# Strided convolution with group norm and GELU, forward and backward: products without matmuls of zeros, five more split leaves, a finer first chunk

## The chip, the cores and the metric

The kernel runs on one core of one Trainium2 chip. The metric is the device time of one execution in microseconds (us); lower is better. The time shown is the median of three executions. One more execution was taken with the hardware profiler; the durations below are from that one.

## The reference

Two sequences of 16000 rows and 256 channels (bf16) go through a strided convolution, a normalisation over time for each sequence and channel, and GELU. The second half of the work is the gradient for all four inputs.

```python
B, T, D, K = 2, 16000, 256, 31
s = 2
L = (T - K) // s + 1                                   # 7985
h = jnp.einsum('blc,cd->bld', x[:, 0:s * L:s, :], w[0])
for i in range(1, K):
    h = h + jnp.einsum('blc,cd->bld', x[:, i:i + s * L:s, :], w[i])
mu = jnp.einsum('bld->bd', h)[:, None, :] / L
var = jnp.einsum('bld->bd', (h - mu) ** 2)[:, None, :] / L
h = (h - mu) / jnp.sqrt(var + 1e-5)
h = h * gn_gamma[None, None, :] + gn_beta[None, None, :]
out = gelu(h, approximate=True)
# reference(): out, and the gradients of x, w, gn_gamma, gn_beta for a given grad_out
```

## The kernel before

The three convolutions (forward, gradient of the input, gradient of the weights) are computed by a fast scheme in the manner of Karatsuba, nested. Tap index and time index are both split by their low bits. At each level four products are replaced by three: one of the "A" parts, one of the "C" parts, and one "B" product of differences or sums, which is added to one and subtracted from the other. Two levels give nine combinations of (branch, leaf), each out of A, B and C. A third level can be applied to a leaf; a leaf to which it is applied is called split here. A leaf that is not split is one long sum of matmuls (`f_leaf`, `g_leaf`, `w_leaf`). A split leaf has three parts: one product of a pair, which TensorE makes once and ScalarE copies to both halves of a PSUM tile with a sign (`f_three_b`, `f_outer`, `g_three_b`, `g_outer`, `w_pairs`), and two further products added on top (`f_three_ac`, `g_three_ac`, `w_single`). That takes three quarters of the matmul columns of the whole leaf, and additional sums or differences on VectorE.

**PSUM.** There are four tiles `ring[0]` to `ring[3]`, each of two banks of 512 fp32 columns. A matmul with the start flag begins a bank anew, and later matmuls into that bank add to it. In `f_three_b` and `w_pairs` the product takes only one half of each bank; one matmul of zeros (weights and data from the zero tile `zt2`) starts each bank before them, writing the other half. The product of one bank is then copied to its own other half, both banks in one ScalarE instruction (L604, L1440).

**Stages.** F is the forward pass (`forward`, matmuls recorded at L572), over 2 batches x 4 chunks x 3 branches. F0 is batch 0 and F1 is batch 1; beside F1 runs the elementwise work of batch 0 (`gelu_batch`, `gelu_unit`). G is the input gradient (`input_grad`, L1103), beside which run the elementwise work of batch 1, the preparation `e_load`, `e_comp`, `dn_turn` of each chunk's gradient, and `d2_piece`, which prepares differences of the gradient for the last stage and writes them to DRAM. W is the weight gradient (`weight_grad`, L1359): nine combinations n = 0 to 8 in turn, with the PSUM pairs X = ring[0:2] and Y = ring[2:4].

**One combination of W.** `x_tile` builds four tiles of x (two blocks of 16384 rows, called b = 0 and 1, in two halves each) by adding raw loads (`w_add`, L1322). `XSUM` is the sum of the two halves for each batch (L1322 as well), `pair_x` (L1419) adds neighbouring rows of a tile, `pair_d` (L1427) and `leaf_d` (L1483) take differences of the gradient. The B product is always split: `w_pairs` into X, then `w_single` into X. Its result seeds the A leaf (in Y) and the C leaf (in X), by a copy or by a VectorE sum with an earlier result (`ve`, L647). Then the two leaves are computed, and `w_done` stores or keeps their results (`w_emit`, L1391). A leaf is split when (n, leaf) is in `NODES`:

```python
NODES = {(0, C_), (6, A), (6, C_), (7, A), (8, C_)}
```

The pair sums of a split leaf live in the buffers `PD`. For n < 2 there are two sets ("all" and "early"), for n > 5 two ("all" and "late"), and for n = 2 to 5 only "all", which the B product uses too. `XSUM` of batch 0 and the temporary of a seed share addresses in some combinations.

**One step of F.** `f_sums` gives the operands (L540). The B leaf is always split except in the very first step. In batch 0 (the set `FO`) the outer leaves A and C are split too, with the weight differences `WD`, the ScalarE copies of `f_outer` (L637) into `TS`, and three operand buffers `U`; in batch 1 they are whole leaves. `f_seed` (L647, L651) adds the results of the B branch.

**The first chunk.** Rows of x are loaded in three pieces (`rows[0]`, `rows[1]` of 128, `rows[2]` of 16) and one half of the chunk is transposed by TensorE against an identity (`x_first`): slot by slot, each with the transposes of both large pieces; then VectorE (L495) and ScalarE (L493) copy the results out. `f_first` makes the first weight differences (`w_sub`, L530) and the first sums before the first leaf.

**Order.** Each instruction is recorded by `add` with its reads and writes and a due time. A planner (`Plan.listing`) runs a list of ready instructions per engine by due time and writes all in the resulting order. The due times follow the order of TensorE's work; `lead` shifts them by kind and stage, `slack` by a constant, `look` limits how far TensorE's groups may be exchanged, `pads` delay what depends on transfers, `hold` ties a piece to a place in TensorE's order, and `PACE` gives the due times of the elementwise units. Each engine and each DMA queue then works strictly in this order. All large transfers are issued by SyncE (SP).

Lines that the text names: L403 loads and stores, L408 DMA transposes, L530 `w_sub`, L540 sums of F, L572 matmuls of F, L604 copy of `f_three_b`, L637 copies of `f_outer`, L647 and L651 VectorE sums of seeds, L655 ScalarE copies (`keep`), L1003 and L1006 elementwise step of a chunk of gradient on VectorE, L1009 and L1011 the same on ScalarE, L1103 matmuls of G, L1266 differences in `d2_piece`, and in W L1322 `w_add`, L1359 matmuls, L1391 `w_emit`, L1419 `pair_x`, L1427 `pair_d`, L1440 copy of `w_pairs`, L1483 `leaf_d`.

Of the kernel before, what the change touches and what calls it, by code (L numbers as in the profile page):

```python
# [38 lines left out]
class Plan:  # L39
# [3 lines left out]
    def __init__(self, tc):  # L43
# [5 lines left out]
        self.slack = 20.0  # L49
        self.hold = -1  # L50
        self.look = 14
        self.pads = (582.0, 557.0, 161.0)
        self.lead = {
            "F0 f_mm f_leaf": -5.0,
            "F0 f_mm f_outer": -6.5,
            "F0 f_mm f_three_ac": -5.5,
            "F0 f_mm f_three_b": -9.0,
            "F0 f_outer forward": 7.5,
            "F0 load put": -14.0,
            "F0 tt f_sums": 7.5,  # L60
            "F0 tt third": -3.0,
            "F0 turn x_load": -10.5,
            "F0 ve f_seed": -4.5,
            "F1 f_mm f_three_ac": 4.0,
            "F1 gelu_unit gelu_batch": 1.5,
            "F1 load gelu_unit": 4.0,
            "F1 tt f_sums": 2.0,
            "F1 tt gelu_unit": -3.5,
            "F1 tt second": 4.0,
            "F1 tt third": -4.0,  # L70
            "F1 ve f_seed": 4.0,
            "G0 g_mm g_leaf": 1.0,
            "G0 g_mm g_three_ac": 1.0,
            "G0 g_mm g_three_b": 1.5,
            "G0 keep g_evac": -3.5,
            "G0 load dn_turn": -17.0,
            "G0 load e_load": 9.5,
            "G0 load g_evac": -3.5,
            "G0 load load_w2": -4.0,
            "G0 spread e_comp": 7.5,  # L80
            "G0 tiny elem_finalize": -8.0,
            "G0 turn dn_turn": 1.5,
            "G0 zero e_comp": 2.0,
            "G1 e_comp conv_stem_kernel": -6.0,
            "G1 g_mm g_leaf": -2.0,
            "G1 g_mm g_outer": 4.5,
            "G1 g_mm g_three_b": 4.5,
            "G1 g_outer input_grad": 2.5,
            "G1 keep g_evac": -2.0,
            "G1 keep g_seed": 10.0,  # L90
            "G1 load d2_piece": 1.0,
            "G1 load dn_turn": 17.0,
            "G1 load e_load": -4.0,
            "G1 load g_evac": 8.5,
            "G1 spread e_comp": -8.5,
            "G1 sub d2_piece": -2.5,
            "G1 tt first": 3.0,
            "G1 tt second": -4.5,
            "G1 turn dn_turn": -2.5,
            "G1 ve g_seed": -1.0,  # L100
# [226 lines left out]
def conv_stem_kernel(  # L327
# [1243 lines left out]
    for br in (B_, C_, A):  # L1571
        load_w2(br)
# [68 lines left out]
```

## Time and profile before

| | |
|---|---|
| median of three executions | 1219.03 us (1217.96 to 1220.42) |
| profiled execution | 1218.8 us, span 1217.0 us, granted TensorE clock 1.00 |
| busy: TensorE / VectorE / ScalarE / GpSimd | 1186.9 / 992.4 / 580.7 / 23.0 us |
| stage F, first to last matmul | 4.7 to 441 us |
| stage G | 441 to 879 us |
| stage W | 879 to 1213 us |
| DMA | 263.55 MB, 16 engines busy 76% of the span |

In the rows, PE is TensorE's matmul, PEld its weight load, DVE is VectorE, ACT is ScalarE, POOL is GpSimd and SP is SyncE. Matmuls overlap in the array, so one matmul's own duration is longer than the distance to the next. A group's row has the number of instructions after x, then the busy time and the mean duration of one in ns. Windows are in us from the span's start.

### The profile page before, as it was taken

The page shows a single profiled execution, that of the slowest core. Times are in us where ns is not written, and L with a number is a line of the kernel's source. Part 1 is how long each engine was busy: PE and PEld are TensorE (multiplying, and loading weights), DVE is VectorE, ACT ScalarE, POOL GpSimd, SP SyncE. Part 2 cuts the span into 40 slices and gives each one's busy share as a digit, 9 for nine tenths or more (in the row PEclk, how much of TensorE's full clock was granted, in tenths as well). Part 3 has the DMA queues.
Part 4 walks back from the last instruction along what each step waited for, and adds up shares of the span by engine and source line. Part 5 has one row for each costly group of instructions (what it writes and reads, how often), then busy time and mean ns, then how long its engine had stood idle before and what let it go on. Part 6 is the DMA issues. An engine that isn't in the chain of part 4 may idle for free.

```text
span 1217.0 us, 19291 instructions
## 1 busy us (share of the span) xinstructions
PE 1186.9 (98%) x7782; PEld 767.1 (63%) x7846; DVE 992.4 (82%) x1265; ACT 580.7 (48%) x801; POOL 23.0 (2%) x68
## 2 busy tenths in 40 slices
PE   6999999999999999999999999999999999999998
PEld 4888889777776974444444444444466665566865
DVE  6988787789999748999885697988785976879883
ACT  1243343478886358878776775544421121112200
POOL 1000000000000000101000000000000000000000
PEclk9999999999999999999999999999999999999999
DMA  9457638758976987685735799998899798897562
GB/s 207 71 158 143 163 96 171 181 130 193 207 188 163 315 296 179 207 241 161 231 117 153 198 323 312 289 336 268 285 249 337 230 322 274 265 334 248 180 177 65
DMA packets 344931, 263.55 MB, mean 217 GB/s; under 512 B 187068, under 2 KB 324538, under 8 KB 336570
## 3 DMA queue, kind: packets, MB, share of 16 engines
q1 hardware_dynamic: 344586, 262.31, 75.7%
q8 instruction: 61, 1.00, 0.3%
q14 instruction: 28, 0.23, 0.1%
q0 software_dynamic: 256, 0.00, 0.0%
HBM read 129.44 MB, written 87.52 MB: 178 GB/s over the span
## 4 chain that ended last, share of the span: by engine, by line
PE 83%; DVE 6%; ACT 4%; DMA 4%; issue 2%; SPq 0%; another core or an unknown queue 0%; POOL 0%; DVEq 0%; ACTq 0%; POOLq 0%
PE ps L572 28%; PE ps L1103 28%; PE ps L1359 26%; DMA arena<-in_x_dram 2%; DVE arena L530 2%; ACT arena L675 1%; DVE arena L540 1%; DVE arena L1266 1%; DMA arena<-dnd 1%; DMA d2d<-arena 1%; DVE arena L914 1%; DVE ps L647 1%; ACT arena L688 1%; ACT arena L1009 1%; DVE arena L647 0%
## 5 line engine op out<-in xcount | busy, mean ns | idle before, releaser
L572 PE MATMUL ps<-arena 128*128 128x256 bf16 (+4 forms) x3552 | 425.3, 281 | 15.4 <-DMA arena<-in_x_dram 9.0
L1103 PE MATMUL ps<-arena 128*128 128x512 bf16 (+1 forms) x1975 | 429.8, 376 | 5.4 <-DVE ps L647 2.1
L572 PEld LDWEIGHTS <-arena 128*128 128x128 bf16 x3552 | 346.9, 98 | 92.8 <-issue 10.7
L1103 PEld LDWEIGHTS <-arena 128*128 128x128 bf16 x2016 | 197.4, 98 | 237.1 <-issue 6.3
L1359 PE MATMUL ps<-arena 128*128 128x256 bf16 (+1 forms) x2153 | 331.6, 313 | 2.0 <-DVE arena L1483 0.5
L655 ACT ACTIVATE arena<-ps 128x1024 f32<-128x1024 f32 (+1 forms) x143 | 145.6, 1020 | 302.3 <-PE ps L1359 76.8
L1359 PEld LDWEIGHTS <-arena 128*128 128x128 bf16 x2176 | 212.9, 98 | 113.4 <-issue 1.2
L540 DVE TENSOR_TENSOR arena<-arena 128x1088 bf16<-128x1088 bf16 (+3 forms) x194 | 163.2, 882 | 14.5 <-PE ps L572 14.2
L914 DVE TENSOR_TENSOR arena<-arena 128x1024 bf16<-128x1024 bf16 x160 | 106.7, 685 | 14.0 <-ACT arena L906 7.9
L1322 DVE TENSOR_TENSOR arena<-arena 128x4096 bf16<-128x4096 bf16 x42 | 95.5, 2285 | 25.3 <-PE ps L1359 18.4
L647 DVE TENSOR_TENSOR ps<-ps,arena 128x1024 f32<-128x1024 f32 x77 | 93.5, 1225 | 27.1 <-PE ps L1359 11.7
L1062 DVE TENSOR_TENSOR arena<-arena 128x516 bf16<-128x516 bf16 (+3 forms) x176 | 82.3, 507 | 10.9 <-PE ps L1103 10.7
L675 ACT ACTIVATE arena<-ps 128x512 bf16<-128x512 f32 (+1 forms) x64 | 37.0, 580 | 87.7 <-PE ps L572 87.6
L1266 DVE TENSOR_TENSOR arena<-arena 128x768 bf16<-128x768 bf16 (+3 forms) x112 | 65.9, 636 | 10.9 <-DMA d2d<-arena 5.6
L647 DVE TENSOR_TENSOR ps<-arena,ps 128x1024 f32<-128x1024 f32 x43 | 52.6, 1224 | 11.5 <-ACT arena L637 4.6
L1483 DVE TENSOR_TENSOR arena<-arena 128x2304 bf16<-128x2304 bf16 x36 | 47.9, 1349 | 13.2 <-PE ps L1359 13.2
L1440 ACT COPY ps<-ps 128x512 f32<-128x512 f32 x28 | 16.0, 572 | 83.7 <-PE ps L1359 83.7
L647 DVE TENSOR_TENSOR arena<-arena 128x1024 f32<-128x1024 f32 x32 | 38.8, 1220 | 15.1 <-ACT arena L1140 7.2
L904 DVE SCALAR_TENSOR_TENSOR arena<-arena 128x1024 bf16<-128x1024 bf16 x32 | 39.0, 1218 | 7.1 <-ACT arena L902 7.0
L530 DVE TENSOR_TENSOR arena<-arena 128x2048 bf16<-128x2048 bf16 (+1 forms) x45 | 42.3, 979 | 0.7 <-DMA arena<-vl 0.7
L924 ACT ACTIVATE arena<-arena 128x1024 bf16<-128x1024 bf16 x32 | 33.6, 1050 | 15.3 <-DVE arena L914 15.3
L900 ACT ACTIVATE arena<-arena,stats 128x1024 bf16<-128x1024 bf16 x32 | 39.3, 1229 | 2.0 <-issue 1.2
(81 smaller groups left out, 627.7 us busy)
## 6 DMA issues: line engine op xcount, KB each, us to landing
arena<-in_x_dram SPq DMA_DIRECT2D x52, 1024.0 KB, 10.3
arena<-d2d SPq DMA_DIRECT2D x16, 1216.0 KB, 11.5
out_dram<-arena SPq DMA_DIRECT2D x14, 1024.0 KB, 5.4
d2d<-arena SPq DMA_DIRECT2D x30, 384.0 KB, 4.8
arena<-dnd SPq DMA_DIRECT2D x10, 960.0 KB, 8.7
vl<-arena SPq DMA_DIRECT2D x36, 256.0 KB, 2.5
arena<-vl SPq DMA_DIRECT2D x9, 1024.0 KB, 8.0
hd<-arena SPq DMA_DIRECT2D x8, 1024.0 KB, 6.0
```

The source lines that it names most:

```text
L530: add("DVE", dve(n), [o], [a, b], lambda: nc.vector.tensor_tensor(out=o, in0=a, in1=b, op=ALU.subtract))
L540: lambda: nc.vector.tensor_tensor(out=o, in0=a, in1=b, op=ALU.add))
L572: yield nc.tensor.matmul(ps[:, dh, cs], lhsT=wt, rhs=mv, start=s0, stop=False, skip_group_check=True)
L647: add("DVE", dve(1024, 1), [out], [a, b], lambda: nc.vector.tensor_tensor(out=out, in0=a, in1=b, op=op))
L655: lambda: nc.scalar.activation(out=out, in_=ps, func=ACT.Copy, scale=scale))
L675: lambda o=o, i=i, ac=ac: nc.scalar.activation(out=o, in_=i, func=ACT.Copy, accum_out=ac))
L914: add("DVE", dve(1024), [o], [a, b_], lambda: V.tensor_tensor(out=o, in0=a, in1=b_, op=op))
L1062: lambda: nc.vector.tensor_tensor(out=o, in0=a, in1=b, op=ALU.add))
L1103: yield nc.tensor.matmul(ps[:, e, 0:wide], lhsT=lt, rhs=mv, start=s0, stop=False, skip_group_check=True)
L1266: lambda: nc.vector.tensor_tensor(out=out, in0=a, in1=b_, op=ALU.subtract))
L1322: add("DVE", dve(4096), [o], [a, b], lambda: nc.vector.tensor_tensor(out=o, in0=a, in1=b, op=ALU.add))
L1359: yield nc.tensor.matmul(ps[:, s, c0:c1], lhsT=lt, rhs=mv, start=s0, stop=False, skip_group_check=True)
```

## The change

Seven things change; the rest of the code is the same.

1. In `f_three_b` and `w_pairs` both halves of the product go side by side into the first bank of the PSUM tile, the first matmul with the start flag. The matmuls of zeros are gone. Three ScalarE copies of 256 columns then fill the second bank and the first bank's other half; before, it was one copy of 2 x 256. `f_outer` takes its weight differences and its temporary as arguments.
2. `NODES` gets the A leaves of n = 1 to 5.
3. In batch 1's last chunk the outer leaves of all three branches are split. Six weight differences are made for that (`f_again`) in addresses of their own.
4. The first chunk: all transposes of the first piece of x stand ahead of those of the second, the small last copy goes from VectorE to ScalarE, the first weight difference and the first sum are made in two halves, the first leaf starts with one half of its taps, and the weights are loaded in another order. The loads of gamma and beta and four stores of zeros move from the start to the second chunk.
5. The elementwise step of batch 1's first chunk moves from ScalarE to VectorE; for its other chunks ScalarE does it in halves.
6. The seven `d2_piece` of batch 0 are spread from the last chunk of batch 0 on, two at a time; before, they began with batch 1.
7. `PACE`, `slack`, `look`, `pads`, the transfer costs and the table `lead` get new values (the table is left out below).

```diff
-        self.slack = 20.0
+        self.slack = 60.0
-        self.look = 14
-        self.pads = (582.0, 557.0, 161.0)
+        self.look = 11
+        self.pads = (1348.0, 1420.5, 1031.5)
...
     def f_three_b(ps, br, lf, op, co):
+        jobs = []
         for dh in range(2):
-            jobs = [(dh, slice(HM, 512), zt2[:, 0:P], zt2[:, 0:HM], True)]
             for q2 in range(2):
                 for par in range(2):
                     for ch in range(2):
                         o0 = (2 * par + ch) * XM + co + q2
-                        jobs.append((dh, slice(0, HM), WD[br, lf][:, ch, q2, par, dh * P:(dh + 1) * P],
-                                     op[:, 1, o0:o0 + HM], False))
-            f_mm(ps, jobs, [ps[:, dh]], [WD[br, lf], op[:, 1], zt2[:]])
-        add("ACT", act(512), [ps[:]], [ps[:]],
-            lambda: nc.scalar.activation(out=ps[:, :, HM:512], in_=ps[:, :, 0:HM], func=ACT.Copy, scale=-1.0))
+                        jobs.append((0, slice(HM * dh, HM * dh + HM), WD[br, lf][:, ch, q2, par, dh * P:(dh + 1) * P],
+                                     op[:, 1, o0:o0 + HM], dh + q2 + par + ch == 0))
+        f_mm(ps, jobs, [ps[:, 0]], [WD[br, lf], op[:, 1]])
+        for o, i, sc in ((ps[:, 1, 0:HM], ps[:, 0, HM:512], 1.0), (ps[:, 1, HM:512], ps[:, 0, HM:512], -1.0),
+                         (ps[:, 0, HM:512], ps[:, 0, 0:HM], -1.0)):
+            add("ACT", act(256), [o], [i],
+                lambda o=o, i=i, sc=sc: nc.scalar.activation(out=o, in_=i, func=ACT.Copy, scale=sc))
...
     def x_first(flat, rows):
...
-        for j, slot in ((0, 2), (1, 3), (2, 0), (3, 1)):
-            ps = ring[slot]
-            for dh in range(2):
-                pe_turn(ps, dh, [(256 * (r % 2) + P * g, g, P, j, r) for r in (2 * dh, 2 * dh + 1) for g in range(2)])
+        slots = (2, 3, 0, 1)
+        for g in range(2):
+            for j in range(4):
+                for dh in range(2):
+                    pe_turn(ring[slots[j]], dh, [(256 * (r % 2) + P * g, g, P, j, r) for r in (2 * dh, 2 * dh + 1)], g == 0)
+        for j in range(4):
+            ps = ring[slots[j]]
...
-        put("DVE", flat.rearrange("p (j o r) f -> p j o r f", j=4, o=2)[:, :, 1, :, 256:XM],
+        put("ACT", flat.rearrange("p (j o r) f -> p j o r f", j=4, o=2)[:, :, 1, :, 256:XM],
...
-    FO = {(0, c, br) for c in range(NCK) for br in ORDER if c or br != B_}
+    FO = {(0, c, br) for c in range(NCK) for br in ORDER if c or br != B_} | {(1, 3, br) for br in FLAST}
...
+    def f_again():
+        zero(U[2][1][:, F - 1:F], 1, "DVE")
+        for br in FLAST:
+            for lf in (A, C_):
+                v = W[br][:, lf]
+                w_sub(WD1[br, lf], v[:, :, 1:4:2], v[:, :, 0:4:2])
...
     def f_first(xt):
         for sl in (A, C_):
             for ch in range(2):
-                w_sub(W[B_][:, sl, ch], W[C_][:, sl, ch], W[A][:, sl, ch])
+                for v in ([slice(None)] if ch or sl == C_ else [0, 1]):
+                    w_sub(*(W[br][:, sl, ch, :, v] for br in (B_, C_, A)))
...
+    EDVE = {(0, 0), (0, 1), (0, 2), (0, 3), (1, 0)}
...
-            if b == 0:
+            if (b, c) in EDVE:
...
-    NODES = {(0, C_), (6, A), (6, C_), (7, A), (8, C_)}
+    NODES = {(0, C_), (1, A), (2, A), (3, A), (4, A), (5, A), (6, A), (6, C_), (7, A), (8, C_)}
...
     def w_pairs(ps, h, pd, ds, om, step):
         jobs = []
         for s in range(2):
             so = 2 * h + s
-            jobs.append((s, 0, D, zt2[:, 0:P], zt2[:, 0:D], True))
             for b in range(NB):
                 for f in range(4):
-                    jobs.append((s, D, 512, pd[b][0][:, f, so * P:(so + 1) * P], ds[b][:, om + step * f, :], False))
-        w_mm(ps, jobs, [ps[:]], [zt2[:], pd[0][0], pd[1][0], ds[0], ds[1]])
-        add("ACT", act(512), [ps[:]], [ps[:]], lambda: nc.scalar.copy(out=ps[:, :, 0:D], in_=ps[:, :, D:512]))
+                    jobs.append((0, s * D, s * D + D, pd[b][0][:, f, so * P:(so + 1) * P], ds[b][:, om + step * f, :], s + b + f == 0))
+        w_mm(ps, jobs, [ps[:, 0]], [pd[0][0], pd[1][0], ds[0], ds[1]])
+        for o, i in ((ps[:, 1, 0:D], ps[:, 0, D:512]), (ps[:, 1, D:512], ps[:, 0, D:512]), (ps[:, 0, D:512], ps[:, 0, 0:D])):
+            add("ACT", act(256), [o], [i], lambda o=o, i=i: nc.scalar.copy(out=o, in_=i))
...
-    D2AT = {(0, 0): (0, 1, 2), (0, 1): (3, 4), (1, 0): (5, 6)}
-    PACE = ((109.0, 7.0), (327.0, 2.5))
+    D2AT = {(0, 3, 0): (0, 1), (0, 3, 1): (2, 3), (1, 0, 0): (4, 5), (1, 0, 1): (6,)}
+    PACE = ((212.0, 40.0), (546.0, 7.0))
```

233 lines of the change are left out of this document (131 added, 102 removed).

## The prediction

> **What bounds the kernel now.** I read the busy row first, then who made TensorE wait, then the spacing of back-to-back matmuls in the chain and the timeline, then the stages.
>
> ```profile
> PE 1186.9 (98%) x7782; PEld 767.1 (63%) x7846; DVE 992.4 (82%) x1265; ACT 580.7 (48%) x801; POOL 23.0 (2%) x68
> ```
>
> TensorE (PE) is busy for all but 30.1 of 1217.0 us. The view of waits, for PE alone, says who caused the larger part of that:
>
> ```profile
> PE ps L572 <- DMA arena<-in_x_dram: 9.0, 2, 4.7
> ...
> PE ps L572 <- DVE arena L530: 3.1, 1, 3.1
> PE ps L572 <- ACT ps L604: 2.8, 3, 1.1
> PE ps L1103 <- DVE ps L647: 2.1, 3, 1.0
> ...
> PE ps L1359 <- DVE arena L1483: 0.5, 1, 0.5
> ```
>
> The waits for DMA and for L530 are the start (12.1 us); afterwards PE hardly waits. But "busy" can hide slack, so the spacing matters. One run of 512-column matmuls from the chain, then 256-column ones from the timeline, among them a matmul of zeros:
>
> ```profile
> 471.69 10.74 PE ps L1103 x49
> ```
> ```profile
> 39.70 0.27 PE L572 MATMUL ps<-zt 128*128 128x256 bf16 x1
> 39.81 1.04 PE L572 MATMUL ps<-arena 128*128 128x256 bf16 x8
> ...
> 40.80 8.05 PE L572 MATMUL ps<-arena 128*128 128x256 bf16 x72
> ```
>
> One 512-column matmul lasts 0.379 us, so 48 spacings take 10.36 us: 0.216 us each. The 72 narrow ones give (8.05 - 0.27) / 71 = 0.1095. A matmul of zeros (zt) moves its successor by 0.11 (39.70 to 39.81), as any other of its width. PE time is therefore columns, 0.109 per 256, and PE is full. Now busy times by stretch: five of one combination each (n = 1 to 5 of the weight gradient), then most of the second batch's forward pass. Behind the stretch and its length stand PE, PEld, DVE, ACT and POOL, then granted clock, DMA share and GB/s:
>
> ```profile
> 915.00:954.00 39.00, 38.84 (x235) 23.09 (x237) 24.49 (x19) 8.01 (x9) 0.00 (x0) 1.00 0.97 316
> 954.00:992.00 38.00, 37.84 (x224) 22.05 (x226) 36.24 (x27) 5.16 (x7) 0.00 (x0) 1.00 0.86 259
> 992.00:1031.00 39.00, 38.84 (x240) 23.68 (x242) 21.04 (x16) 7.82 (x9) 0.00 (x0) 1.00 0.89 302
> 1031.00:1070.00 39.00, 38.84 (x227) 22.24 (x229) 32.26 (x24) 5.15 (x6) 0.00 (x0) 1.00 0.83 268
> 1070.00:1108.00 38.00, 37.84 (x215) 21.24 (x217) 30.54 (x23) 4.09 (x5) 0.00 (x0) 1.00 0.87 284
> ```
> ```profile
> 212.00:330.00 118.00, 116.89 (x897) 87.37 (x897) 104.57 (x154) 86.31 (x128) 0.31 (x1) 1.00 0.81 180
> 330.00:441.00 111.00, 108.71 (x922) 89.80 (x921) 92.01 (x143) 63.89 (x106) 3.18 (x9) 1.00 0.84 235
> ```
>
> VectorE (DVE) is the second-fullest engine throughout, at 36.2 of 38 in n = 2. That is where a gain will be lost.
>
> **What leaves PE.** Counts are from the two built programs.
> - Zeros: 46 in the forward pass and 56 in the weight gradient, 102 x 0.109 = 11.1 us.
> - Five leaves: 64 matmuls of 512 (13.8 us) become 96 of 256 (10.5 us), 3.3 each, 16.6 in all.
> - Last forward chunk: 92 of 231 and 96 of 230 columns go; by the two spacings such a one is 0.0985 (estimate), 18.5 us; 96 of 256 come, 10.5. Net 8.0.
>
> Sum 35.7 us. Each narrow matmul needs its own weight load; the PEld groups have 98 ns each, below 109, so loads stay hidden.
>
> A rule speaks against the second item. The Trainium skill, "TensorE: Matmul & The Clock Gate", section "Back-to-back issue gap", gives a sustained spacing, in streams of weight load and matmul, of about 131 ns at 512 columns and 81 ns at 128, and calls 216 ns the isolated gap. Between its two figures 256 columns would be about 98 ns (estimate from that page), so a split leaf would go from 8.4 to 9.4 us and lose 1.0. Here 49 matmuls in a row show 216 ns, so the trace disagrees.
>
> **What this puts on VectorE.** A split leaf adds two L1419 (1.217 us in the groups by form), four L1427 (0.683) and two L647 (1.22): 7.6 us, or 7.0 as neighbours overlap by about 0.08 (a 1.22 us one at 15.05 is followed at 16.18). PE's period falls by 3.3 + 0.44 (four zeros) to some 34.8. In n = 2 to 5 VectorE needs 36.24 + 21.04 + 32.26 + 30.54 + 28.0 = 148.1 us; PE needs 154 - 15.1 = 138.9. VectorE becomes the bound by 9.2 us. Stretch n = 1 has 35.2 - 31.5 = 3.7 spare, of which I take half to be usable: L1322 of n = 3 is written over tiles that n = 1 still reads. VectorE also waits in this stage for DMA (5.9 us) and for the ACT copies L1440 (10.7 us); some of that stays when it is full. I add 3. So PE stalls about 10 us here (bounds 4 and 18), mainly at a combination's first products (waiting for L1322 and L1419) and at the seeds (L647).
>
> The last forward chunk adds six weight differences L530 (1.22), twelve sums L540 (0.72), six L647 (1.22): 23.2, some 21.3 with overlap. The two forward rows hold 196.6 us of DVE; 218 then stands against PE's 229 - 8.0 - 2.6 (24 zeros of this batch) = 218.4. No slack is left. Before, VectorE waited here 13.2 us for PE, which vanishes when it is late, and 10.2 for ACT; half of the latter remains: 5 us of new PE waits (0 to 10).
>
> **ACT copies.** Each product's copy of 512 (0.58 in F, 0.57 in W) becomes three of 256, not shown by the trace. Between half of 0.58 and all of it, three cost 0.87 to 1.74; the rows of 1024 (1.02) and 512 give 0.35 each, near the low end, 1.06. So a product is finished 0.5 later. The 23 forward ones made PE wait three times (2.8 us); elsewhere other groups stood between. +1.0, bounds 0 and 8.
>
> **Start.**
>
> ```profile
> 9.26 4.01 PE L572 MATMUL ps<-arena 128*128 128x128 bf16 x47 [4.31 <-DMA arena<-in_x_dram]
> 10.22 1.22 DVE L495 CAST arena<-ps 128x1024 bf16<-128x1024 f32 x1 [8.62 <-PE ps L572]
> ...
> 13.30 0.42 DVE L495 CAST arena<-ps 128x256 bf16<-128x256 f32 x1 [0.15 <-PE ps L572]
> 13.84 1.29 DVE L540 TENSOR_TENSOR arena<-arena 128x2176 bf16<-128x2176 bf16 x1
> 15.05 1.22 DVE L530 TENSOR_TENSOR arena<-arena 128x2048 bf16<-128x2048 bf16 x1
> ```
>
> Only one transpose runs ahead of the second piece of x. With all of the first piece's ahead, the first cast moves from 10.22 to about 9.7, the second then ends at 12.1; the 0.42 cast goes to ACT behind its second copy (12.2 to 12.6). The sums start near 12.6 instead of 13.84. VectorE is without a gap from there to 49 us, so its 1.2 us is what counts, not the earlier first matmul. Bounds: gain 2.5, loss 1 (weights now land in another order).
>
> **At nothing.** The elementwise step of batch 1, chunk 0 on VectorE (+3.1 us, L1003 and L1006) and the other ACT steps in halves (24 of about 1.23 for 12 of 2.04, +5 us): DVE has 20 of 115 us free in 655 to 770, ACT 98 of 224 in 655 to 879. The d2 pieces of batch 0 begin one chunk earlier: 56 L1266 (33 us), 7 loads, 35 stores; 441 to 655 has 38 us of free DVE and a DMA share of 0.61, but in SP's queue the first of them now stand ahead of two transposes (dn_turn) of batch 1's chunk 0 and of the loads of its chunk 1, for which VectorE and then PE would wait. The gamma/beta loads and four zero stores leave the start for the second chunk, later elementwise due times and new planner weights shuffle the rest. If that cover fails it is the 3.1 us by which PE is already idle in 655 to 770, twice over; I keep 3 us either way.
>
> **Sum.** 1217.0 - 35.7 + 10 + 5 + 1 - 1.2 = 1196.1 us of span. The profiled execution took 1218.8, 1.8 beyond its span, and the median of the runs is 1219.03, another 0.2: 1198 us. About 0.2% (2.4 us) is what a measurement can tell from no change.
>
> **Rivals.**
> - All of it arrives: VectorE work is pulled ahead into n = 0 and n = 1 and into the forward pass's idle 13 us of 212 to 330, no new waits: 1217.0 - 35.7 - 1.2 = 1180, time 1182. For: DVE rose to 29.8 of 30 us in 300 to 330 without a PE wait. Against: the 148.1 over 138.9. 0.10 for this end, up to 1189.
> - VectorE binds harder: its waits for ACT and DMA all stay, stalls at their upper bounds of 18, 10 and half of the copies' 8: 1217 - 35.7 + 32 - 1.2 = 1212, time 1214. 0.10.
> - Slower: in n = 2 to 5 the split leaf has only the one buffer set that the first products use, so L1419 must wait for those products and L1427 for the singles, and VectorE's queue holds the next tile's L1322 and the next L1419 behind them. Were PE's singles (64 x 0.109 = 7.0 us) and 32 of products (3.5) exposed in full each time, four combinations lose 42: 1217 - 35.7 + 42 + 6 - 1.2 = 1228, time 1230. It decides from about 8 us per combination, (35.7 + 1.2 - 6) / 4. Against: two L1483 and an L1322 stand ahead of L1419 in the built order, so the products are done by then. 0.07 for all slower ends; 0.03 for within 0.2%.
> - Wide matmuls turn out cheaper per column in these streams, and the five leaves give nothing: 16.6 of the gain go, but VectorE then needs 148.1 against 154 - 1.8 = 152.2 and about 7 of the 10 us of stalls go too: 1196 + 16.6 - 7 = 1206, time 1208. The 10.74 us row leaves it 0.01, counted in the forecast's own range. It is what the page of the Trainium skill named above would make of this kernel.
>
> The forecast case keeps 0.70. Faster 0.90, same 0.03, slower 0.07. The range 1184 to 1212 reaches from nearly the full gain to the harder bound and leaves out some 0.18.
>
> **What would show it.** PE busy near 1151; no matmul of zt; 256-column rows still at 0.109. In the weight gradient, n = 2, 4 and 5 last 37 to 39 us with DVE above 95%, PE waiting for L1322, L1419 and L647 (by their new numbers), while n = 1 and 3 shorten to 35 or 36. The forward pass shows a few PE waits on DVE in its last chunks. The first DVE sum starts near 12.6. I am wrong in the main point if DVE has more than 5% idle in n = 2 to 5 while PE has none (gain too small), or if PE idles over 25 us beyond the start.

## The result and the profile after

The changed kernel takes 1190.65 us (median of four executions, 1190.54 to 1192.69), the kernel before on the same chip 1218.74 us (1217.96 to 1220.42). The ratio is 0.9772, with a 95% interval of 0.9755 to 0.9789: 28.1 us less, where the prediction had 20.9. The profiled execution has a span of 1188.7 us, 28.3 less than before.

Lines have moved. In the changed kernel matmuls stand in L585 (forward), L1141 (input gradient) and L1398 (weight gradient); `w_sub` is L540, sums of the forward pass L550, the VectorE sums of seeds L663 and L667, `keep` L671, the copy that ends a forward seed L691, the product copies L620 and L1479, x tiles L1361, pair sums L1458 and L1466, the d2 differences L1305. The experiments move lines by a few more: L1398 is L1400 or L1401 in some of them, and in plan_old every line number is one less (L1397, L1140, L584).

The busy row of the page, which answers to the first one shown of before:

```profile
PE 1155.4 (97%) x7812; PEld 763.7 (64%) x7812; DVE 1048.4 (88%) x1335; ACT 616.3 (52%) x953; POOL 27.7 (2%) x69
```

TensorE's busy time falls by 31.5 us and VectorE's rises by 56.0. TensorE now idles 33.3 us of its span; before it was 30.1. The waits of PE say where (line, what it waited for, us in total, times, the longest):

```profile
PE ps L585 <- DMA arena<-in_x_dram: 6.4, 2, 4.7
PE ps L1141 <- DVE ps L663: 5.8, 4, 2.6
PE ps L585 <- DVE arena L540: 4.6, 2, 2.8
PE ps L585 <- ACT arena L691: 3.0, 3, 2.0
PE ps L1398 <- ACT arena L671: 2.9, 3, 1.7
PE ps L1398 <- DVE ps L663: 2.5, 3, 1.6
PE ps L1141 <- ACT ps L1168: 1.8, 2, 1.6
PE ps L1398 <- ACT ps L1479: 1.3, 1, 1.3
```

All waits together are 29.2 us, against 22.7 before. The first and third row are the start (11.0 us; 12.1 before). The weight gradient has 6.7 (0.8 before), the input gradient 8.6 (3.2 before), and the forward pass behind its start 3.0 (6.7 before). No row names L620, the new copies of the forward products.

The stretches answer to the tables of before: the second batch's forward pass in two, the first batch's input gradient, and n = 1 to 6 of the weight gradient, about one combination each. Behind each stretch and its length stand PE, PEld, DVE, ACT, POOL, then granted clock, DMA share and GB/s:

```profile
212.00:330.00 118.00, 114.96 (x849) 83.10 (x847) 105.75 (x156) 92.44 (x139) 0.31 (x1) 0.99 0.81 176
330.00:430.00 100.00, 100.00 (x827) 80.57 (x825) 97.93 (x144) 65.72 (x122) 3.30 (x10) 1.00 0.82 229
430.00:655.00 225.00, 223.88 (x1051) 102.71 (x1050) 204.00 (x328) 174.92 (x201) 10.56 (x24) 1.00 0.74 220
...
902.00:937.00 35.00, 35.00 (x262) 25.42 (x260) 28.66 (x25) 10.27 (x19) 0.00 (x0) 1.00 1.01 331
...
937.00:972.00 35.00, 33.17 (x249) 24.14 (x247) 35.00 (x27) 8.59 (x17) 0.00 (x0) 1.00 0.78 238
972.00:1007.00 35.00, 35.00 (x259) 25.14 (x257) 34.73 (x30) 10.44 (x18) 0.00 (x0) 1.00 1.06 356
1007.00:1045.00 38.00, 37.18 (x269) 26.15 (x268) 37.64 (x33) 7.55 (x16) 0.00 (x0) 1.00 0.95 311
1045.00:1084.00 39.00, 35.30 (x259) 25.07 (x257) 39.00 (x33) 8.34 (x17) 0.00 (x0) 1.00 0.91 296
1084.00:1116.00 32.00, 32.00 (x295) 28.69 (x294) 32.00 (x32) 13.90 (x26) 0.00 (x0) 1.00 0.66 211
```

From 937 to 1084 us, n = 2 to 5, VectorE has 0.63 us free in 147. PE has 6.4 us free there, most of it in n = 2 and n = 5, where VectorE has no gap at all. In n = 6 both are full and PE does not wait, and in n = 1 VectorE still has 6.3 us free. In the last 100 us of the forward pass PE is full, VectorE is busy for 97.9, and PE does not wait. The third row stands against this one of before. VectorE's busy share there rises from 0.82 to 0.91: 14 of the d2 differences now lie in it (9.1 us), and the gradient, further on at the same time, does 85 of its own sums L1100 where it did 57:

```profile
441.00:655.00 214.00, 212.16 (x1001) 99.78 (x1020) 175.82 (x276) 176.36 (x199) 8.74 (x21) 1.00 0.61 186
```

By the first and last matmul of each stage the forward pass ends 15.6 us earlier (445.6 to 430.0), the weight gradient begins 12.2 earlier (879.5 to 867.3), and it ends 28.3 earlier (1213.15 to 1184.85).

### The profile page after: what moved, and what is told of

Read it like the earlier page. It is cut to its first block, busy times and chain, and to the rows that moved or that the text cites. A ratio compares the mean times of both kernels' runs of the same rounds, so it can differ in the third digit from the quotient of the medians.

```text
span 1188.7 us, 19509 instructions
## 1 busy us (share of the span) xinstructions
PE 1155.4 (97%) x7812; PEld 763.7 (64%) x7812; DVE 1048.4 (88%) x1335; ACT 616.3 (52%) x953; POOL 27.7 (2%) x69
## 4 chain that ended last, share of the span: by engine, by line
PE 67%; DVE 14%; DMA 7%; ACT 4%; issue 4%; SPq 3%; DVEq 0%; POOL 0%; ACTq 0%
PE ps L585 31%; PE ps L1398 18%; PE ps L1141 17%; DMA arena<-hd 2%; DVE arena L1361 2%; DVE arena L948 2%; SPq L412 2%; DVE ps L663 2%; DVE arena L1305 2%; SPq L407 1%; DMA arena<-d2d 1%; DMA d2d<-arena 1%; DVE arena L1100 1%; DMA arena<-dnd 1%; ACT arena L1047 1%
## 5 line engine op out<-in xcount | busy, mean ns | idle before, releaser
L1141 PE MATMUL ps<-arena 128*128 128x512 bf16 (+1 forms) x2016 | 432.7, 376 | 8.7 <-DVE ps L663 5.8
L585 PE MATMUL ps<-arena 128*128 128x256 bf16 (+4 forms) x3460 | 412.8, 282 | 14.0 <-DMA arena<-in_x_dram 6.4
L585 PEld LDWEIGHTS <-arena 128*128 128x128 bf16 x3460 | 338.1, 98 | 88.7 <-DMA arena<-in_x_dram 6.6
L1141 PEld LDWEIGHTS <-arena 128*128 128x128 bf16 x2016 | 197.1, 98 | 243.1 <-issue 11.8
L1398 PE MATMUL ps<-arena 128*128 128x256 bf16 (+1 forms) x2336 | 310.9, 296 | 6.7 <-ACT arena L671 2.9
L1398 PEld LDWEIGHTS <-arena 128*128 128x128 bf16 x2336 | 228.5, 98 | 89.1 <-issue 8.1
L671 ACT ACTIVATE arena<-ps 128x1024 f32<-128x1024 f32 (+1 forms) x147 | 149.4, 1020 | 252.8 <-PE ps L1141 88.7
L550 DVE TENSOR_TENSOR arena<-arena 128x1087 bf16<-128x1087 bf16 (+3 forms) x207 | 172.5, 876 | 12.6 <-PE ps L585 11.9
L948 DVE TENSOR_TENSOR arena<-arena 128x1024 bf16<-128x1024 bf16 x160 | 107.5, 690 | 16.1 <-ACT arena L940 9.8
L663 DVE TENSOR_TENSOR ps<-ps,arena 128x1024 f32<-128x1024 f32 x82 | 99.9, 1231 | 21.4 <-ACT ps L1479 14.4
L1361 DVE TENSOR_TENSOR arena<-arena 128x4096 bf16<-128x4096 bf16 x42 | 95.6, 2293 | 2.7 <-PE ps L1141 2.2
L1479 ACT COPY ps<-ps 128x256 f32<-128x256 f32 x114 | 40.7, 357 | 103.8 <-PE ps L1398 101.4
L1100 DVE TENSOR_TENSOR arena<-arena 128x516 bf16<-128x516 bf16 (+3 forms) x176 | 83.2, 514 | 9.2 <-PE ps L1141 7.9
L1305 DVE TENSOR_TENSOR arena<-arena 128x768 bf16<-128x768 bf16 (+3 forms) x112 | 66.2, 640 | 15.3 <-DMA arena<-dnd 9.7
L691 ACT ACTIVATE arena<-ps 128x512 bf16<-128x512 f32 (+1 forms) x64 | 36.9, 578 | 71.0 <-PE ps L585 70.9
L663 DVE TENSOR_TENSOR ps<-arena,ps 128x1024 f32<-128x1024 f32 x44 | 54.0, 1227 | 8.1 <-PE ps L1141 5.1
L663 DVE TENSOR_TENSOR arena<-arena 128x1024 f32<-128x1024 f32 x36 | 43.6, 1223 | 11.1 <-ACT arena L1178 5.5
L1466 DVE TENSOR_TENSOR arena<-arena 128x1024 bf16<-128x1024 bf16 x76 | 49.8, 697 | 1.8 <-DMA arena<-d2d 1.7
L540 DVE TENSOR_TENSOR arena<-arena 128x2048 bf16<-128x2048 bf16 (+1 forms) x52 | 50.0, 997 | 0.5 <-DMA arena<-in_w_dram 0.5
L653 ACT ACTIVATE arena<-ps 128x512 f32<-128x512 f32 x56 | 29.2, 606 | 37.1 <-PE ps L585 37.1
L1458 DVE TENSOR_TENSOR arena<-arena 128x2048 bf16<-128x2048 bf16 x38 | 45.5, 1229 | 0.0
```

The source lines that it names most:

```text
L540: add("DVE", dve(n), [o], [a, b], lambda: nc.vector.tensor_tensor(out=o, in0=a, in1=b, op=ALU.subtract))
L550: lambda: nc.vector.tensor_tensor(out=o, in0=a, in1=b, op=ALU.add))
L585: yield nc.tensor.matmul(ps[:, dh, cs], lhsT=wt, rhs=mv, start=s0, stop=False, skip_group_check=True)
L663: add("DVE", dve(1024, 1), [out], [a, b], lambda: nc.vector.tensor_tensor(out=out, in0=a, in1=b, op=op))
L671: lambda: nc.scalar.activation(out=out, in_=ps, func=ACT.Copy, scale=scale))
L948: add("DVE", dve(1024), [o], [a, b_], lambda: V.tensor_tensor(out=o, in0=a, in1=b_, op=op))
```

## The experiments

Each was timed in five rounds with the kernel before on the same chip, whose median there was 1218.8, 1219.5 and 1219.1 us. Differences below are of medians, against 1190.65. A "gap" is a stretch in which PE waits.

### The zeros put back, at two widths (z256, z512)

```diff
# in f_mm and w_mm, before the first matmul of a product (two of them, 122 in all)
+                for _ in range(zeros if s0 else 0):
+                    yield nc.tensor.matmul(ps[:, s, 0:256], lhsT=zt2[:, 0:P], rhs=zt2[:, 0:256], start=False, stop=False, skip_group_check=True)
# z512: 0:512 in place of 0:256
```

> The changed kernel with two matmuls of zeros of 256 columns put back into every product of a pair (46 in the forward pass, 76 in the weight gradient), the order of all other instructions kept; zeros are added, so nothing else changes. My theory (TensorE is bound by columns, 0.109 us per 256): +13.3 us of PE work, of which up to 1.7 us falls into the waits of n = 2 to 5, so +11.6 to +13.3 us over the changed kernel's 1190.7. Rival (PE has hidden slack between narrow matmuls): under +6. The Trainium skill's sustained spacing, interpolated to 98 ns, would give +12.0, which this run can't tell from mine.

> As z256 with zeros of 512 columns instead of 256. My theory (0.216 us each in a stream of weight loads and matmuls): 122 x 0.216 = +26.4 us, 24 to 26.4 over 1190.7. Rival (a wide matmul is cheaper per column when it is pipelined with others): by the Trainium skill's sustained spacing of 131 ns it would be +16.0, so under +18.

Measured: 1201.38 us (1200.88 to 1204.67), +10.7, and 1213.02 us (1211.23 to 1214.46), +22.4. PE's timeline where a product begins in the weight gradient, first z256, then z512:

```profile
871.60 0.38 PE L1402 MATMUL ps<-zt 128*128 128x256 bf16 x2
871.82 1.91 PE L1400 MATMUL ps<-arena 128*128 128x256 bf16 x16
```
```profile
875.83 0.59 PE L1402 MATMUL ps<-zt 128*128 128x512 bf16 x2
876.26 1.91 PE L1400 MATMUL ps<-arena 128*128 128x256 bf16 x16
```

Two zeros of 256 columns move what follows by 0.22 us (871.60 to 871.82), two of 512 by 0.43 (875.83 to 876.26): 0.11 and 0.215 each, so twice the columns cost twice the time. The sums close as well: 122 x 0.109 = 13.3 us, less 3.1 us of waits that the later PE no longer had (26.1 in all, from 29.2), is 10.2 against 10.5 of span. For z512 it is 26.2 less 3.1 of waits and less 1.7 for a dip of the clock that it did not have (explained below), 21.4 against 21.9 of span. Both times lie under what was expected, because more waits were covered than I allowed for, and in z512 because of the dip; they are far from the rivals' under 6 and under 18. A matmul of zeros costs its columns even where VectorE is near full, less the part of the waits that it covers. The rule of the Trainium skill, "TensorE: Matmul & The Clock Gate", section "Back-to-back issue gap", by which 512 columns would take about 131 ns in such a stream, does not hold here: 0.215 us was measured.

### The five leaves whole again (nodes_old)

```diff
-    NODES = {(0, C_), (1, A), (2, A), (3, A), (4, A), (5, A), (6, A), (6, C_), (7, A), (8, C_)}
+    NODES = {(0, C_), (6, A), (6, C_), (7, A), (8, C_)}
```

> The changed kernel with the old list of split leaves (the A leaves of n = 1 to 5 whole again); the planner orders anew. My theory: +16.6 us of PE work, less some 5 us of waits that VectorE caused, so +10 to +13. Rival (the splits were worth their full columns, the waits belong to something else): +16 to +18. Rival (VectorE ate the gain): under +6.

Measured: 1204.54 us (1202.4 to 1205.88), +13.9. The waits of PE in the weight gradient fall from 6.7 to 3.4 us, with these rows left:

```profile
PE ps L1398 <- ACT arena L671: 2.1, 2, 1.5
PE ps L1398 <- ACT ps L1479: 1.3, 1, 1.3
```

16.6 - 3.3 = 13.3 us, which is the difference of the spans (1202.0 to 1188.7). The planner orders this kernel anew, but the waits of the other two stages stay as they were (14.2 and 8.4 us, against 14.0 and 8.6). The five splits are half of the gain of the change, and VectorE takes back a fifth of what they free on PE.

### Less and more on VectorE in the weight gradient (w_light, w_heavy)

```diff
# w_light: the sums of raw loads for n = 3 to 6 on one of eight row groups
+                w_add(t, t, x_raw(b, k3, k1, k2), 1)
# w_heavy: the sums of two x tiles for n = 2 to 5, each done twice
+                w_add(XSUM[b], xt[b, 0], xt[b, 1], 2 <= n <= 5)
```

> The changed kernel, order kept, but the 20 additions that build the x tiles of n = 3 to 6 work on one eighth of their rows only (so those tiles of x are not complete): VectorE loses 37 us of work in n = 2 to 5. My theory (VectorE's load is what holds PE in n = 2 to 5): PE waits in the weight gradient fall from 6.7 us to 2 or less, -4 to -6 us. Rival 1 (emptying PSUM on ScalarE and its three small copies hold PE): within 1 us of 1190.7, waits for ScalarE stay. Rival 2 (transfers of x hold it): within 2 us, PE or DVE waits for DMA take the place.

> The changed kernel with the eight sums of the outer x tiles of n = 2 to 5 in the weight gradient done twice (a second L1361 over the same operands, the same values; order of all other work kept). It adds 8 x 2.2 = 17.7 us of VectorE work where VectorE is 95 to 100% busy, and none to PE. Theory (VectorE is full in n = 2 to 5 and what is added there reaches the end one for one, less the small gaps it still has): +14 to +17 us over the changed kernel, that is 1204.5 to 1208, with PE waits in the weight gradient rising from 6.7 to over 18 us. Rival (PE still sets the pace there and the 6.7 us of waits are local, from order and buffers): under +6, below 1197.

Measured: w_light 1186.61 us (1184.69 to 1187.16), -4.0; w_heavy 1207.83 us (1206.89 to 1212.39), +17.2. PE's timeline in w_heavy (start, us, ..., in brackets the gap ahead and who ended it):

```profile
939.93 3.37 PE L1401 MATMUL ps<-arena 128*128 128x256 bf16 x16 [4.46 <-ACT arena L671]
944.58 33.19 PE L1401 MATMUL ps<-arena 128*128 128x256 bf16 x238 [1.28 <-ACT ps L1482]
980.55 50.69 PE L1401 MATMUL ps<-arena 128*128 128x256 bf16 x381 [2.79 <-DVE arena L1461]
1034.64 22.65 PE L1401 MATMUL ps<-arena 128*128 128x512 bf16 x125 [3.40 <-DVE ps L663]
1060.68 1.91 PE L1401 MATMUL ps<-arena 128*128 128x256 bf16 x16 [3.40 <-ACT arena L671]
```

VectorE bounds this stage, but only just: 17.7 us added come back as 17.2 (the stage alone goes from 317.6 to 335.7 us, 18.2 more), while 35.0 us taken away (VectorE's busy time goes from 1048.4 to 1013.4) give 4.0, hardly more than the waits lose. These fall from 6.7 to 3.3, not to the 2 or less that was expected: 1.3 us for the product copies L1479 and 2.0 in three short waits stay. So w_heavy excludes its rival, that PE still sets the pace, but half of the 6.7 us does not go away with VectorE's load. The 17.2 us are not all waits, though. PE's waits in the weight gradient rise by 12.9 us; three of these gaps (4.46, 2.79 and 3.40) are each followed by a stretch at half the granted clock. The stretches around the first:

```profile
938.00:940.00 2.00, 0.07 (x1) 0.07 (x1) 2.00 (x2) 1.17 (x2) 0.00 (x0) 0.89 0.94 274
940.00:942.00 2.00, 2.00 (x10) 1.36 (x10) 2.00 (x2) 0.00 (x0) 0.00 (x0) 0.50 0.51 180
942.00:944.00 2.00, 1.30 (x8) 0.83 (x6) 2.00 (x3) 0.58 (x2) 0.00 (x0) 0.76 0.12 40
```

The granted clock is the first number behind the five engines: 0.89, 0.50, 0.76. What is missing to 1, times 2 us each, is 0.22 + 1.00 + 0.48 = 1.7 us. Call this a dip. Four of them (the fourth at 687 us) against one in the changed kernel are 5.1 us; with 12.9 more of waits in the weight gradient, 2.2 less in the input gradient and 0.7 less in the forward pass that makes 15.1, and the spans differ by 15.9.

### The last forward chunk's outer leaves whole again (flast_off), or their VectorE work lightened (f_light)

```diff
# flast_off
-    FLAST, GLAST = ORDER, ()
+    FLAST, GLAST = (), ()
# f_light (and in third(): the sums of outer leaves of batch 1, chunk 3, on an eighth)
-                w_sub(WD1[br, lf], v[:, :, 1:4:2], v[:, :, 0:4:2])
+                w_sub(WD1[br, lf], v[:, :, 1:4:2], v[:, :, 0:4:2], D // 8)
```

> The changed kernel with the outer leaves of the last forward chunk (batch 1, chunk 3) whole again, as in the kernel before; all else of the change stays. PE gets 8.0 us of columns back, VectorE loses some 21 us in the last two chunks of the forward pass. Theory (the split is worth its columns on PE, and the VectorE work it costs was put off into the first batch's gradient, whose PE waits rose from 3.2 to 8.6 us): PE +8.0, waits of the gradient -3 to -5, so +3 to +5 us over the changed kernel: 1193.5 to 1196. Rival A (VectorE's added work costs nothing): +8, 1198 to 1199. Rival B (the 5 us of new PE waits that the prediction gave this edit are there, hidden as VectorE gaps before): 0 to +3.

> The changed kernel, every instruction in its place; of what the split of the last forward chunk's outer leaves adds to VectorE, the six weight differences L540 and the twelve sums are done on one eighth of their elements (the rest of those operands is left out): about 12.5 us of VectorE less between 330 and 430 us. The prediction put this work at 5 us of new PE waits. Theory A (it is absorbed: the work behind it was put off to later places at no cost): 1189.5 to 1191.5, PE waits as before. Theory B (PE does pay for it, in waits that the trace attributes to others, L691 at 250 us or the gradient's first waits): -2 to -5, 1185.5 to 1188.5.

Measured: f_light 1191.32 us (1190.39 to 1192.28), +0.7; flast_off 1206.33 us (1205.04 to 1208.16), +15.7.

f_light takes 11.0 us of work from VectorE (1048.4 to 1037.4), about half of what the split of this chunk adds, and gains nothing:

```profile
PE 1154.9 (97%) x7750; PEld 764.9 (64%) x7812; DVE 1037.4 (87%) x1335; ACT 616.2 (52%) x953; POOL 27.0 (2%) x69
```

Its waits are 2.9 us less (26.3 against 29.2), but the wait of 2.3 us at 701 us is gone behind a second dip of the clock, at 689 us, which costs 1.7 instead, and the wait at 24 us that is 1.3 less lies far ahead of the edit. So this work costs PE nothing that can be seen. flast_off missed every expectation. By stage (profiled spans, +17.1 in all) the forward pass ends 5.3 us later, and the other 11.8 come behind it, where nothing was undone. PE's waits, its first rows:

```profile
PE ps L585 <- DMA arena<-in_x_dram: 6.8, 2, 4.6
PE ps L1141 <- ACT arena L671: 6.2, 3, 3.1
PE ps L1141 <- DVE ps L663: 5.6, 6, 1.8
```

The input gradient's waits (L1141) are 16.9 us, against 8.6. Its work is the same in both; its order is not, because the planner sorts all work anew when the list of work changes. So this kernel prices the split together with an order that its constants were not made for, and cannot price the split alone. The same holds for the next one.

### The d2 pieces back in their old place (d2at_old), or without their wait (d2_nowait)

```diff
# d2at_old
-    D2AT = {(0, 3, 0): (0, 1), (0, 3, 1): (2, 3), (1, 0, 0): (4, 5), (1, 0, 1): (6,)}
+    D2AT = {(1, 0, 0): (0, 1, 2), (1, 0, 1): (3, 4), (1, 1, 0): (5, 6)}
# d2_nowait, in sub() of d2_piece: differences that read the load read a tile of zeros
+            if raw and b == 0 and pc < 4:
+                ra = rb = zt2[:, 0:D].rearrange("p (o d) -> p o d", o=1).to_broadcast([P, out.shape[1], D])
```

> The changed kernel with the second-gradient pieces of batch 0 (d2_piece: 56 L1305 subtractions, 33 us of VectorE, with their loads and stores) put where the kernel before had them, from batch 1's chunk 0 on, instead of from batch 0's chunk 3. Theory (the pieces that now start a chunk earlier are what crowds VectorE between 655 and 760 us, where PE's waits on L663 rose): the gradient's waits fall by 3 to 5 us: 1185.5 to 1187.5. Rival A (the waits come from the forward pass's work that was put off and from the elementwise step of batch 1, chunk 0 on VectorE): within 1.5 us of the changed kernel, 1189 to 1192. Rival B (the earlier start was needed, the later pieces collide with the weight gradient's first loads): +2 or more, over 1192.5.

> The changed kernel, every instruction in its place; only the subtractions of the first four second-gradient pieces of batch 0 (L1305) that read a piece's load read a tile of zeros instead, so that VectorE does not wait there for the load (it waited 5.55 us at 681.53 us, and the seed L663 for which PE then waited 2.62 us at 687.30 stands behind it in VectorE's queue). Those pieces of the weight gradient are left out. Theory (this wait at the head of VectorE's queue is what the earlier pieces cost PE): the waits of the gradient fall from 8.6 to 4 to 6 us, 1186 to 1188.5. Rival (the queue is late for other reasons, the elementwise step and the forward pass's left-over work): the next wait takes its place, within 1 us of the changed kernel, 1189.7 to 1191.7.

Measured: d2at_old 1202.69 us (1200.74 to 1205.37), +12.0, on the side of its rival B, though not by its mechanism (the weight gradient's waits are 7.2 us against 6.7); d2_nowait 1187.89 us (1187.33 to 1191.49), -2.8. In d2at_old the later pieces bring longer gaps in the input gradient (waits 15.5 us, against 8.6), and again half a clock behind them. PE's timeline there, and the stretches around its second gap:

```profile
702.53 0.61 PE L1141 MATMUL ps<-arena 128*128 128x256 bf16 x2 [3.65 <-DVE ps L663]
703.36 27.20 PE L1141 MATMUL ps<-arena 128*128 128x512 bf16 x119 [0.22 <-issue]
734.62 3.57 PE L1141 MATMUL ps<-arena 128*128 128x512 bf16 x8 [4.07 <-ACT arena L671]
739.45 5.88 PE L1141 MATMUL ps<-arena 128*128 128x512 bf16 x18 [1.25 <-DVE ps L663]
```
```profile
734.00:736.00 2.00, 1.38 (x4) 0.55 (x4) 1.98 (x3) 1.48 (x2) 0.00 (x0) 0.50 0.15 48
736.00:738.00 2.00, 2.00 (x6) 0.61 (x5) 2.00 (x4) 0.00 (x0) 0.34 (x2) 0.50 1.05 321
738.00:740.00 2.00, 0.75 (x3) 0.25 (x2) 2.00 (x4) 1.90 (x3) 0.64 (x4) 0.50 0.95 352
740.00:742.00 2.00, 2.00 (x7) 0.63 (x5) 1.23 (x2) 2.00 (x4) 0.37 (x1) 0.50 1.06 161
```

From 734 to 742 us the clock stays at half, and a second gap (1.25 us) falls into the slow stretch. My theory that the earlier pieces crowd the input gradient has fallen: later pieces were worse in the order that these constants give.

In d2_nowait the order is that of the changed kernel, instruction by instruction. The time lies where the theory put it, but the trace does not bear it out: PE's wait at that place falls only from 2.62 to 1.73 us, because the next difference in VectorE's queue then waits 2.77 us for a store of the piece before:

```profile
681.26 1.03 DVE L1308 TENSOR_TENSOR arena<-arena 128x768 bf16<-128x768 bf16 x2 [2.77 <-DMA d2d<-arena]
```

The next wait for L663 stays (2.41 us, 2.28 in the changed kernel), and all waits together are 29.2 us in both. The intervals of the ratios (0.9737 to 0.9764, and 0.9755 to 0.9789) overlap. Three of its five executions have a granted clock of 1.000 and take 1187.3 to 1187.9 us; the other two (0.998), of which the profiled one is the first, take 1190.4 and 1191.5, and the changed kernel's four have 0.997 or 0.998. So most of the 2.8 us can be a dip that did not come. VectorE's wait for this load is worth at most 2.8 us, and what causes the input gradient's waits stays open: no run undoes point 5 of the change, the elementwise step of batch 1.

### The planner's constants (plan_old, leads_old, before_new)

```diff
# plan_old: all constants of the kernel before, in the changed kernel;
# leads_old: only the table of leads; before_new: the new constants in the kernel before
-        self.slack = 60.0
+        self.slack = 20.0
-        self.look = 11
-        self.pads = (1348.0, 1420.5, 1031.5)
+        self.look = 14
+        self.pads = (582.0, 557.0, 161.0)
         self.lead = {
...
-    PACE = ((212.0, 40.0), (546.0, 7.0))
+    PACE = ((109.0, 7.0), (327.0, 2.5))
```

> The changed kernel with the planner's constants (due-time leads per kind of work, slack, look-ahead, pads, pace of the d2 pieces) of the kernel before; the same instructions, ordered by the old constants. The prediction put the new constants at nothing, plus or minus 3. Theory A (the constants only shuffle): 1188 to 1194. Theory B (with VectorE full in n = 2 to 5, the order of its work is what keeps PE's waits at 6.7 us rather than the 10 predicted, and the forward pass at no new waits rather than 5): +4 to +12, 1195 to 1203, with more PE waits on L663 in the weight gradient and on VectorE in the last forward chunks.

> The changed kernel with the old table of leads alone; slack 60, look-ahead 11, pads and pace stay new. With all of them old it took 1306.5. Theory (the table of leads carries most of what the constants are worth, since it decides who goes first on VectorE, ScalarE and SP): 1230 to 1300. Rival (slack, look-ahead and pads carry it: work is put in order of due times that the slack of 60 spreads): under 1215.

> The kernel before, with nothing of the change but the planner's constants (leads, slack, look-ahead, pads, pace). Theory (the constants fit one program's list of work and are no better in general): slower than the kernel before by 15 to 90 us, 1234 to 1310, in new PE waits in all three stages. Rival (they are better constants, and part of the 28 us is theirs): faster than before by 3 us or more, under 1216.

Measured: plan_old 1306.45 us (1304.94 to 1309.37), +115.8 and past all that was expected; leads_old 1294.59 us (1292.49 to 1296.62), +103.9; before_new 1241.87 us (1238.33 to 1244.31), 22.8 slower than the kernel before. PE's longest waits in plan_old:

```profile
PE ps L1140 <- DVE arena L539: 17.2, 1, 17.2
PE ps L1140 <- ACT ps L1167: 11.7, 10, 3.0
PE ps L1397 <- DVE arena L1521: 11.2, 1, 11.2
PE ps L584 <- DVE arena L539: 9.3, 1, 9.3
```

Three of the four are single long gaps: the first matmul of the input gradient stands 17.2 us behind one weight difference that VectorE was given too late. PE's waits sum to 117.8 us, 88.6 more than in the changed kernel, and its busy time for the same matmuls is 1181.4 us, 26.0 more, with a mean granted clock of 0.965: gaps and the half clock behind them. Most hangs on the table of leads (103.9 of 115.8).

before_new closes in the same way: waits 37.3 us against 22.7 in the kernel before, and half-clock dips of 5.1 us, make 19.7, and the spans differ by 19.6. Nearly all of it is in the input gradient (waits 21.7 us, against 3.2), not in all three stages as was expected. The constants are therefore not better in general. Each set fits one list of work, and used on the other it costs 23 us in one direction and 116 in the other. This does not make them the source of the 28 us: they are what lets the 35.7 us that leave PE arrive.

## Why the prediction was right, point by point

The time lay in the range and 7.4 us below the figure. By the prediction's own terms, measured by PE's waits of the two profiled executions:

- **Columns, -35.7.** They hold, though PE's busy time is 1155.4 us and not the 1151 that the prediction named: it falls by 31.5 only. The trace of before has 7782 matmuls beside 7846 weight loads, so 64 records are missing, and the holes of under 0.15 us that they leave are not counted as busy (3.6 us in all, against 0.2 after, where none is missing). And one dip of the clock adds 1.7 us of busy time after. 31.5 + 3.4 + 1.7 = 36.6 us. The zeros cost 0.11 each when put back, the five leaves 13.9 us net, which is 16.6 less the waits they caused. The last forward chunk's 8.0 was not seen alone, because undoing it changed the order of everything behind it; the forward pass by itself lost 5.3.
- **Stalls of the weight gradient, +10.** The mechanism was right: n = 2 to 5 are bound by VectorE, with waits for L663 and for `keep` behind it (at 1043.67 us ScalarE's copy L671 has itself waited 4.65 us for VectorE's `w_emit`, L1430). The size was 5.9 (0.8 to 6.7), near the lower bound of 4, and of it 3.3 to 3.4 went with the splits (nodes_old) or with VectorE's load (w_light). The balance alone, 9.2 less 1.9 for n = 1, would have given 7.3; the mis-sized term is the 3 us for waits that VectorE itself would keep. It was taken from VectorE's waits in the whole stage, 5.9 us for DMA and 10.7 for L1440. In n = 2 to 5 (954 to 1108 us) they were 4.1 and none before the change, and they are 0.2 and 0.4 after it. From first product to first product n = 1 to 5 last 34.8, 36.9, 34.8, 35.8 and 39.0 us, near the lengths forecast.
- **Last forward chunk on VectorE, +5.** This failed; the term was nothing. The added work did come, but between 212 us and the end of the forward pass VectorE is busy for 203.7 us where it was 196.6: 7.1 more, not 21.3. Twelve more sums and four more weight differences stand before 212 us than before the change (VectorE is busy 7.9 us more from 60 to 212; part of it because PE is further on), and 2.8 us of the next stage's preparation moved behind the end. The balance of 218 against 218.4 held the list of work in this stage fixed, and that was the error. f_light shows no cost in the half of the added work that it takes away.
- **ACT copies, +1.** They measured 0.357 us (L1479) and 0.374 (L620), near the 0.35 of the estimate. But no wait for the forward copies is left, where before there were 2.8 us (three times, L604): that part of the term was -2.8, and no run shows what removed them. In the weight gradient one wait of 1.3 us for L1479 is new, in n = 2; it is counted in the 5.9 above, but it stands in nodes_old and w_light too and so belongs here. The forward waits for the seed's copy went from 3.9 to 3.0.
- **Start, -1.2.** The first sum stands at 11.55 us (13.84 before, 12.6 forecast), and the first product follows at 13.57. But half of that is lost again at the next weights:

```profile
11.55 1.36 DVE L550 TENSOR_TENSOR arena<-arena 128x1088 bf16<-128x1088 bf16 x2 [0.31 <-ACT arena L500]
```
```profile
13.57 8.62 PE L585 MATMUL ps<-arena 128*128 128x512 bf16 x48 [2.83 <-DVE arena L540]
23.95 36.31 PE L585 MATMUL ps<-arena 128*128 128x512 bf16 x298 [1.76 <-DVE arena L540]
```

  The waits of the first 60 us fell by 1.1.
- **At nothing, 3 either way.** Two parts of this were wrong. The input gradient's waits rose by 5.4 us, nearly all of it from 655 us on, the place that was named if the cover should fail. And the constants were put here at nothing, which holds only for this pair of program and constants.
- **Not in the sum:** one dip of the clock, 1.7 us, at 252 us, behind a wait of 1.98 us for L691:

```profile
252.00:254.00 2.00, 2.00 (x11) 1.26 (x10) 2.00 (x2) 2.00 (x5) 0.00 (x0) 0.54 0.98 287
254.00:256.00 2.00, 2.00 (x10) 1.02 (x9) 2.00 (x4) 1.87 (x3) 0.00 (x0) 0.61 0.00 0
```

With these in place the sum is -35.7 + 5.9 - 2.8 - 0.9 - 1.1 + 5.4 + 1.7 = -27.5; the spans differ by 28.3, and the columns' 36.6 in place of 35.7 would close the rest. So the figure was too high because too much was charged for stalls in the weight gradient, the last forward chunk and the product copies, more than the input gradient and the clock, charged with nothing, took back: 13.8 us too much in the first (with the seed's copy), 7.1 too little in the second. That half of the error cancelled is luck. That the new constants would fit was taken for granted, not worked out.

Neither of the two signs of being wrong came: VectorE is 0.4% idle in n = 2 to 5, and PE idles 22.3 us beyond its start.

Of the rivals, the first ("all of it arrives", up to 1189) came nearer than the forecast's own figure: 1190.65 is 1.7 us above its end. Its mechanism held in the forward pass, where VectorE's work was pulled ahead and no new wait for it came; its "no new waits" failed in the weight gradient and in the input gradient. "VectorE binds harder" and the slower one through the shared buffers did not come: no PE wait names the pair sums L1458 or L1466. w_heavy shows how near the harder bound was: 17.7 us more of VectorE work in n = 2 to 5 gave 1207.8, towards that rival's 1214. The cheaper wide matmuls are excluded by z512.

## What to carry to other kernels

Where an engine is full, take work off it by columns and price the helper engine's added work by stage: it costs one for one only where nothing can be put off (the weight gradient here), and nothing where the order can do it elsewhere (the forward pass). When a planner with fitted constants sets the order, undoing one part of a change also undoes the fit; compare with the order held, by lightening or repeating single operations, or else by stage and only up to the edit. Count for each longer gap of PE the half clock that may follow it, not only the gap.

## What was not expected of the hardware

**A gap of PE can cost 1.7 us beyond itself.** In twelve profiled executions (both kernels, before_new, and the experiments other than plan_old and leads_old) the granted clock behind the start was set against every gap of 1 us or more. No gap under 1.9 us started a dip. Of 27 gaps from 1.97 to 3.1 us 12 did, and of 6 from 3.4 us up 5. The same gap of 1.97 to 1.98 us at 251 us was followed by a dip in four executions and by none in three others, so in this range the length of the gap does not decide it. A single dip takes 1.7 us of full clock, that is 3.4 us at half. The Trainium skill, "TensorE: Matmul & The Clock Gate", section "What's actually happening", gives a free-running window of about 3.4 us, and half rate after at least one idle window. The length agrees with these rows, and a window that runs free would fit the chance; but here gaps of 2 us, shorter than a window, were enough.

**Half the columns take more than half the time on ScalarE.** A copy of 256 columns from PSUM to PSUM took 0.357 us after the change, one of 512 took 0.572 before: 0.62 of the time.

```profile
L1440 ACT COPY ps<-ps 128x512 f32<-128x512 f32 x28 | 16.0, 572 | 83.7 <-PE ps L1359 83.7
```
```profile
L1479 ACT COPY ps<-ps 128x256 f32<-128x256 f32 x114 | 40.7, 357 | 103.8 <-PE ps L1398 101.4
```
